# Placing score maxima, positive parts and splits in the projection stage by booked engine clocks instead of counted columns

## The chip, the cores and the metric

The kernel runs on one core of a Trainium2 chip. The metric is the device time of one execution, in microseconds (us). A core has TensorE (PE: matrix products, with its weight loads shown as PEld), VectorE (DVE), ScalarE (ACT), GpSimd (POOL) and SyncE (SP, which here only issues DMAs). Each engine works through its own queue in order and waits at an instruction until the semaphores that it needs have been raised. TensorE writes to PSUM, eight banks of 512 float32 columns on 128 partitions.

## The reference

One transformer block on 2048 tokens of 640 values, with 32 heads of 20 values, in float32:

```python
x = A_x
h = x + _A_ref(_layernorm(x), A_wqkv, A_wo)     # attention: softmax(q k^T * 20**-0.5) v, times wo
h2 = h + _B_ref(_layernorm(h), B_w_gate, B_w_up, B_w_down)   # (silu(z @ w_gate) * (z @ w_up)) @ w_down
```

The softmax subtracts the row maximum of the scores, so that maximum has to be known before the exponentials.

## The kernel before

The kernel has three stages. The first (the subject here) takes the layernorm of x, multiplies by wqkv, stores queries, keys and values in HBM, and computes a part of the score maxima ahead of the attention. The second is the attention with the remaining maxima, the third the output projection and the feed-forward part. All products are made in float32 precision from two reduced-precision parts: each operand is split into `hi` and `lo` (`split`, L84: ScalarE copies the value to `hi`, another engine subtracts), and three products hi*hi, lo*hi and hi*lo are summed.

**Work of the first stage.** Tokens come in four chunks of 512 (`c`). Each chunk has 10 query and key blocks (`query_key`, 512 columns wide) and 8 value blocks (`value`, 320 columns wide); `slot` counts them, 18 to a chunk, from 0 to 71. A block is the sum of 15 products (three kinds by five pieces of the 640 inner values). `rounds` (L484) issues each of these as two half matmuls on 64 of TensorE's 128 rows; the first half of one block runs at the same time as the second half of an older one, on the other rows. The second halves stand in the list `behind`: when it holds more than 21, the oldest is issued. Both halves add into the same bank, so after the last first half of a block a marker on VectorE (`clobber_nop`) has to pass before the first of its second halves may start. When a block's last second half is issued, `keep` (L546) or `keep_value` (L596) takes the bank: ScalarE copies it, the split follows, by `split_later` some columns later (ScalarE's copy and GpSimd's subtraction), and the result is stored to HBM by `store` (L469), from GpSimd's queue in most slots. `store` keeps the newest pieces back until the next call, a block later.

**Maxima between the blocks.** `max_pair` (L171) multiplies 128 queries by 512 keys for two heads (two matmuls, two banks) and VectorE reduces each bank to its maximum (L181). `max_four` (L185) does four heads with two reductions only. For two keys a and b, max(a, b) is b plus the positive part of a - b. The stored keys hold the differences of their halves as a third part, so `differences` multiplies the queries by key differences (four matmuls of 256 columns, two banks), ScalarE takes the positive part in place (Relu, L203), and `maxima` adds the products with the plain keys on top (four more matmuls) and VectorE reduces the sums (L208). Such a pair is called a job here. The tiles that a job reads (`raw`, six buffers) are loaded back from HBM by `load_items` (L319) on SP's queue, from a slot on at which the store has been issued (`stored_at`); `ready` (L347) lets a job go some slots after its load was issued. Banks for maxima (`ps_max`) rotate through five, block sums (`ps_one`) through three.

**What sets the order.** Every engine's queue is written out by this program; nothing is reordered later. `visit` (L389) is called after each product of a block, from slot 7 on, and decides whether a job goes in. It counts columns of TensorE work: a job's `maxima` comes `BEHIND` columns after its `differences`, and jobs are spaced by `BETWEEN` and `SPACING`:

```python
BETWEEN, SPACING, BEHIND = 11 * CH // 2, 5 * CH, 13 * CH // 2
```

Jobs stand in two lists, `early` (four heads, staged tiles) and `urgent` (maxima of the first unit, from tiles that stay); `early` goes first up to slot 59. The layernorm of the next chunk (`norm`, L429: statistics, an inverse root in small steps, application, all on VectorE) is taken apart into 15 steps, in the list `lns`, one or two of which are issued after each block. `flip` (L446) transposes the normalized chunk on TensorE. When the blocks are done, the rest of `behind` is issued with a `visit` after each; the maxima of unit 0 are finished by `max_finish` (L236), which the attention needs.

Of the kernel before, what the change touches and what calls it, by code (L numbers as in the profile page):

```python
# [17 lines left out]
P = 128  # L18
# [26 lines left out]
def tile_block(ctx: ExitStack, tc: tile.TileContext, x, wqkv, wo, wg, wu, wd, out):  # L45
# [123 lines left out]
    mxs = {u: stk.tile([P, 2, 2, TPC, NC], F32, name=f"mx{u}") for u in range(NU)}  # L169

    def max_pair(mx, q, k, pair, t, kc, k0):  # L171

        banks = [ps_max() for _ in range(2)]
        for b, ps in enumerate(banks):
            rows = slice(b * ROW, b * ROW + NPART)
            nc.tensor.matmul(  # L176
                ps, q[rows, pair, t * P : (t + 1) * P], k[rows, pair, k0 : k0 + CH],
                start=True, stop=True,
            )
        for b, ps in enumerate(banks):  # L180
            nc.vector.tensor_reduce(  # L181
                mx[:, b, pair, t, kc : kc + 1], ps, axis=AX.X, op=ALU.max
            )

    def max_four(mx, q, k, t, kc):  # L185
# [4 lines left out]
        def products(cols, first):  # L190
            for pair in range(2):
                for b in range(2):
# [5 lines left out]
                    )  # L198

        def differences():  # L200
            products(slice(half, CH), True)
            for ps in banks:
                nc.scalar.activation(ps, ps, AF.Relu)  # L203

        def maxima():
            products(slice(0, half), False)
            for b, ps in enumerate(banks):
                nc.vector.tensor_reduce(  # L208
                    mx[:, b, :, t, kc], ps.rearrange("p (j n) -> p j n", j=2),
                    axis=AX.X, op=ALU.max,  # L210
                )
# [73 lines left out]
    with tc.tile_pool(name="pa", bufs=2) as pa:  # L285
# [33 lines left out]
        def load_items():  # L319
            for n, (which, g, c, loaded, _) in enumerate(items):  # L320
# [10 lines left out]
                stack(t, which, g, c, slice(CH // 2, EW) if which else slice(0, CH))  # L331
                items[n][3:] = t, slot[0]

        def staged_keys(g, c, kc, k, q):
            def four(t):
                first, second = max_four(mxs[g * NC + c], items[q][3], items[k][3], t, kc)

                def last():
                    second()
                    for n in (k, q):  # L340
                        users[n] -= 1
                    load_items()

                first()
                return last

            def ready():  # L347
                return all(items[n][3] is not None and slot[0] >= items[n][4] + 2 + (slot[0] < 24) for n in (k, q))

# [35 lines left out]

        columns, due, seconds = [0], [0], []
        BETWEEN, SPACING, BEHIND = 11 * CH // 2, 5 * CH, 13 * CH // 2

        def visit():  # L389

            load_items()
            if seconds and columns[0] >= seconds[0][0]:
                columns[0] += CH
                seconds.pop(0)[1]()
            if columns[0] < due[0]:
                return
            for queue in (early, urgent) if slot[0] < 60 else (urgent, early):
                if queue and queue[0][0]():
                    columns[0] += CH
                    last = queue.pop(0)[1]()  # L400
                    if last:
                        seconds.append((columns[0] + BEHIND, last))
                    due[0] = max(due[0] + BETWEEN, columns[0] + SPACING)
                    return
            due[0] = max(due[0], columns[0] - 4 * BETWEEN)

# [12 lines left out]
        def split_w(m):  # L419
            cs = slice(m * P, (m + 1) * P)  # L420
            split(raws.pop(m), w_hi[:, :, cs], w_lo[:, :, cs])

        def z_tiles(c):
# [22 lines left out]
        def flip(c, k):  # L446
            if k == 0:
                zs[c] = z_tiles(c)
            ps = ps_max()
            for t in range(TPC):  # L450
                nc.tensor.transpose(  # L451
# [22 lines left out]

        behind, splits = [], []

        def second_half():
            if behind:
                f, done = behind.pop(0)
                f(1)  # L480
                if done:
                    done()

        def rounds(ps, n_columns, operands, done):  # L484

            last = len(operands) - 1
            for n, (a, b) in enumerate(operands):

                def half(i, n=n, a=a, b=b):
# [17 lines left out]

# [15 lines left out]

        def split_later(f):
            splits.append((columns[0] + 7 * CH, f))

# [19 lines left out]
        def keep(c, m, ps):  # L546

            finish_splits()
            e = next_e()
            which, half, n = 1 - m % 2, CH // 2, CH  # L550
# [3 lines left out]
            if slot[0] < 10:  # L554
                if which:
# [3 lines left out]
                    )  # L559
                split(ps, hi[:, :CH], lo[:, :CH], nc.vector)  # L560
                if which:
                    split_later(lambda: split(over, hi[:, CH:], lo[:, CH:], nc.gpsimd))
            else:
                nc.scalar.activation(copy[:, :CH], ps, AF.Copy)
                if which and c < 2:
# [30 lines left out]
        def keep_value(c, t, half, ps):  # L596
            finish_splits()
            ev = evs[t % 2]
            dst = ev[:, half * 4 : half * 4 + 4, : G * VW].rearrange("p g (h w) -> p g h w", h=G)
# [41 lines left out]
        for c in range(NC):  # L641
# [7 lines left out]
            for j, (kind, *which) in enumerate(work):  # L649
# [27 lines left out]
                else:  # L677
                    ps_ctx.close()
                    ps_ctx = ExitStack()
                    psum = ps_ctx.enter_context(  # L680
                        tc.tile_pool(name="psum_p", bufs=1, space=bass.MemoryType.PSUM)
                    )

                    def ps_one():
                        return psum.tile([P, CH], F32, name="ps_one", tag="ps_one", bufs=3)

                    def ps_max():
                        return psum.tile([P, CH], F32, name="ps_max", tag="ps_max", bufs=5)

# [1084 lines left out]
```

## Time and profile before

| | us |
|---|---|
| median of 3 runs (lowest, highest) | 2088.42 (2087.58, 2092.59) |
| the profiled execution | 2087.61 |
| its span, first to last instruction | 2085.5 |
| TensorE busy in the span | 2049.9 |
| VectorE busy | 1642.5 |
| ScalarE busy | 1440.5 |
| GpSimd busy | 744.3 |
| end of the last projection matmul, from the start of the span | 372.1 |

The span lies 2.1 us below the profiled execution's time; the rest is before its first and after its last instruction. In the rows below, a name like `ps_max<-raw,raw` tells the tile that is written and those that are read, L194 the line of the program, x4 that four instructions are merged, and `[0.51 <-DVE mx L208]` that the engine stood idle for 0.51 us before the row and what ended that. Rows of windows give, for each engine, the time it was busy in the stretch and the number of its instructions, then the granted TensorE clock as a share of full speed, the share of the DMA engines and GB/s. Rows of waits give who waited for whom, the sum in us, the count and the longest. Rows of grouped instructions give the count, busy us and mean ns of one, and after the second bar the idle time of the engine ahead of them. A busy TensorE is not one at its peak: overlapping matmuls, one of which is held up, count as busy.

### The profile page before, as it was taken

How to read it: one execution, taken by the hardware profiler on the slowest of the kernel's cores; microseconds unless marked ns; L12 is line 12 of the kernel's file. 1: busy time of each engine (PE TensorE's matmuls, PEld its weight loads, DVE VectorE, ACT ScalarE, POOL GpSimd, SP SyncE). 2: the span in 40 equal slices, each digit the busy share in tenths (PEclk: the TensorE clock that was granted, in tenths of full speed). 3: DMA queues.
4: the chain of work that ended last, by engine and by line, in shares of the span. 5: the costliest groups of instructions: out<-in, count | busy, mean ns of one | idle time of the engine just before them, and what ended most of it. 6: DMA issues, size and time to landing. Idle time of an engine off the chain costs nothing.

```text
span 2085.5 us, 39669 instructions
## 1 busy us (share of the span) xinstructions
PE 2049.9 (98%) x14198; PEld 1251.5 (60%) x14198; DVE 1642.5 (79%) x2895; ACT 1440.5 (69%) x2835; POOL 744.3 (36%) x1039
## 2 busy tenths in 40 slices
PE   7989999999999999999999999999999999999999
PEld 6878788433333433333333333335588888888888
DVE  6757878798888888888888888886368676676667
ACT  3657774899999999999999999996743222212221
POOL 2353423334342434353510001001145444753556
PEclk9999999999999999999999999999999999999999
DMA  6766553253354443534521213131138755884542
GB/s 216 234 205 187 180 162 107 64 159 109 128 155 128 140 125 122 168 124 154 177 100 58 52 32 98 31 117 61 35 123 291 249 182 176 307 300 156 196 155 95
DMA packets 192300, 305.53 MB, mean 146 GB/s; under 512 B 47440, under 2 KB 82256, under 8 KB 191080
## 3 DMA queue, kind: packets, MB, share of 16 engines
q1 hardware_dynamic: 185576, 278.87, 41.6%
q0 software_dynamic: 6432, 24.12, 3.8%
q8 instruction: 113, 1.85, 0.4%
q14 instruction: 83, 0.68, 0.1%
q10 hardware_dynamic: 96, 0.00, 0.0%
HBM read 203.82 MB, written 98.30 MB: 145 GB/s over the span
## 4 chain that ended last, share of the span: by engine, by line
PE 91%; DMA 4%; DVE 2%; issue 1%; ACT 1%; SPq 1%; POOL 0%; DVEq 0%; ACTq 0%; POOLq 0%
PE acc L1076 24%; PE ps_one L1066 16%; PE ps_a L1237 14%; PE ps_max L219 12%; PE ps_one L491 9%; PE ps_b L1331 7%; PE ps_max L194 4%; PE ps_max L797 2%; PE ps_b L797 1%; DVE mx L208 1%; DMA halves<-j_d 1%; DMA raw<-q_d 1%; DMA t<-t_d 1%; PE ps_max L451 0%; PE ps_max L176 0%
## 5 line engine op out<-in xcount | busy, mean ns | idle before, releaser
L1072 ACT ACTIVATE probs<-ps_one 128x512 f32<-128x512 f32 x2048 | 1056.8, 616 | 62.7 <-PE ps_one L1066 38.5
L225 DVE TENSOR_REDUCE mx<-ps_max 128x1 f32<-128x512 f32 x1472 | 925.7, 683 | 115.2 <-PE ps_one L1066 77.1
L1066 PE MATMUL ps_one<-q_stk,k_stk 62*128 62x512 f32 x2048 | 585.5, 450 | 2.6 <-DVE m L86 1.8
L1076 PE MATMUL acc<-probs,v_stk 128*32 128x512 f32 x4096 | 545.7, 605 | 0.0
L1066 PEld LDWEIGHTS ps_one<-q_stk,k_stk 62*128 62x128 f32 x2048 | 251.5, 184 | 432.4 <-ACT probs L1072 397.8
L219 PE MATMUL ps_max<-k_stk,q_stk 60*128 60x512 f32 x1472 | 382.6, 425 | 0.0
L219 PEld LDWEIGHTS ps_max<-k_stk,q_stk 60*128 60x128 f32 x1472 | 271.8, 186 | 24.7 <-DVE mx L225 1.1
L1452 DVE TENSOR_TENSOR tmp<-ps_a,tmp 128x512 f32<-128x512 f32 x208 | 141.1, 689 | 120.5 <-PE ps_a L1237 94.7
L208 DVE TENSOR_REDUCE mx<-ps_max 128x2 f32<-128x512 f32 x256 | 164.7, 686 | 67.9 <-PE ps_max L194 51.7
L1111 POOL TENSOR_TENSOR o<-o,rb 128x512 f32<-128x512 f32 x31 | 40.0, 1290 | 407.8 <-DMA q_stk<-q_d 174.1
L1076 PEld LDWEIGHTS acc<-probs,v_stk 128*32 128x32 f32 x4096 | 80.5, 108 | 173.8 <-issue 165.3
L1331 PE MATMUL ps_b<-halves,yp 128*128 128x320 f32 x1032 | 179.3, 308 | 1.9 <-DMA halves<-j_d 1.4
L1331 PEld LDWEIGHTS ps_b<-halves,yp 128*128 128x128 f32 x1032 | 165.1, 188 | 18.5 <-POOL yp L86 1.5
L203 ACT ACTIVATE ps_max<-ps_max 128x512 f32<-128x512 f32 x256 | 137.2, 579 | 55.5 <-PE ps_max L194 52.1
L1237 PE MATMUL ps_a<-t,units 128*128 128x512 f32 x624 | 162.5, 396 | 0.0
L1237 PE MATMUL ps_a<-z,units 128*128 128x512 f32 x516 | 133.8, 394 | 0.0
L86 POOL TENSOR_TENSOR yp<-y,yp 128x256 fp32r<-128x256 f32 x96 | 60.2, 627 | 188.0 <-ACT yp L85 188.0
L1237 PEld LDWEIGHTS ps_a<-t,units 128*128 128x128 f32 x624 | 112.6, 188 | 18.6
L491 PE MATMUL ps_one<-z_hi,w_hi 64*128 64x512 f32 x380 | 117.7, 407 | 3.8 <-DVE z_lo L86 2.5
L491 PE MATMUL ps_one<-z_lo,w_hi 64*128 64x512 f32 x380 | 117.7, 404 | 0.0
L491 PE MATMUL ps_one<-z_hi,w_lo 64*128 64x512 f32 x380 | 115.4, 400 | 0.0
L1336 DVE TENSOR_TENSOR h<-ps_b,h 128x320 f32<-128x320 f32 x248 | 109.9, 480 | 6.8 <-PE ps_b L1331 5.4
(201 smaller groups left out, 2699.7 us busy)
## 6 DMA issues: line engine op xcount, KB each, us to landing
units<-w_d SPq DMA_DIRECT2D x186, 256.0 KB
w_d<-stage SPq DMA_DIRECT2D x106, 256.0 KB
halves<-j_d SPq DMA_DIRECT2D x70, 320.0 KB
j_d<-stage SPq DMA_DIRECT2D x42, 320.0 KB
k_stk<-k_d SPq DMA_DIRECT2D x64, 160.0 KB
q_stk<-q_d SPq DMA_DIRECT2D x64, 160.0 KB
raw<-k_d SPq DMA_DIRECT2D x54, 160.0 KB
rb<-r_d SPq DMA_DIRECT2D x32, 256.0 KB
```

The lines of the kernel that those rows point to most:

```text
L203: nc.scalar.activation(ps, ps, AF.Relu)
L208: nc.vector.tensor_reduce(mx[:, b, :, t, kc], ps.rearrange("p (j n) -> p j n", j=2), axis=AX.X, op=ALU.max,)
L219: nc.tensor.matmul(ps, queries[u][rows, pair, t * P : (t + 1) * P], keys[u // NC][rows, pair, kc * CH : (kc + 1) * CH], start=True, stop=True,
L225: nc.vector.tensor_reduce(mxs[u][:, b, pair, t, kc : kc + 1], ps, axis=AX.X, op=ALU.max)
L491: nc.tensor.matmul(ps, a[rows], b[rows], start=(i == n == 0), stop=(i == 1 and n == last), skip_group_check=True,)
L1066: nc.tensor.matmul(ps, keys[u // NC][rows, p, kt * P : (kt + 1) * P], queries[u][rows, p, :], start=True, stop=True,)
L1072: nc.scalar.activation(probs[p][:, b, :], ps, AF.Exp, scale=scale)
L1076: nc.tensor.matmul(acc[32 * j : 32 * j + 32, :], values[u // NC][:, kt, j * VW : j * VW + 32], probs[j // 2][:, j % 2, :], start=(kt == 0) ...
L1237: nc.tensor.matmul(ps.rearrange("p (t n) -> p t n", t=TPC), w[k][:, i], z[k][:, :, j], start=(first and m == 0), stop=(last and m == len(n ...
L1331: nc.tensor.matmul(ps, a, b, start=(n == 0), stop=(n == len(pairs) - 1))
L1336: nc.vector.tensor_tensor(out=h, in0=ps, in1=h, op=ALU.add)
L1452: add = lambda out, ps, x: nc.vector.tensor_tensor(out=out, in0=ps, in1=x, op=ALU.add)
```

## The change

The column counts are replaced by four clocks in ns, one for each engine, kept while the program is written. `takes` books work on an engine: the work starts at that engine's clock or when its input is ready, whichever is later. `held` is the list of times at which the five maxima banks come free.

- A job's `differences` books 240 on PE and two Relus of 478 on ACT; its `maxima` goes when PE's clock has reached the end of the Relus plus 150, and books two reductions of 600 on DVE, which set when its two banks come free.
- `visit` starts a new job only when PE's clock has reached the time at which the second of the next two banks comes free and ACT's clock is no more than 500 ahead. It also issues a waiting split when its time has come and ACT is no more than 200 ahead, and (from slot 9 on) a norm step when DVE is no more than 100 ahead. It is called in every slot.
- Loads count as landed 8000 of PE's clock after `load_items` issued them (12000 up to slot 23), instead of two or three slots later.
- In most slots a block's store is issued right after its split instead of at the next block.
- Second halves follow after 19 instead of 21 products. `urgent` goes first from slot 57 instead of 60.
- The five and three banks come from two pools instead of one. The last loop also runs while jobs are left, and `max_finish` follows the loop if it has not been issued.

```diff
+    clock = dict.fromkeys(("PE", "ACT", "DVE", "POOL"), 0)
+    held = [[0] for _ in range(5)]
+    RELU = 150
+
+    def takes(engine, ns, ready=0):
+        clock[engine] = max(clock[engine], ready) + ns
+        return clock[engine]
+
+    def hold(*until):
+        held[: len(until)] = []
+        held.extend(until)
...
     def max_pair(mx, q, k, pair, t, kc, k0):
...
+        done = takes("PE", 240)
         for b, ps in enumerate(banks):
             nc.vector.tensor_reduce(
                 mx[:, b, pair, t, kc : kc + 1], ps, axis=AX.X, op=ALU.max
             )
+            hold([takes("DVE", 600, done + 205) + 100])
...
+        until = [[1e9] for _ in banks]
+
         def differences():
             products(slice(half, CH), True)
+            done = takes("PE", 240)
             for ps in banks:
                 nc.scalar.activation(ps, ps, AF.Relu)
+                takes("ACT", 478, done + 150)
+            hold(*until)
+            return clock["ACT"] + RELU
 
         def maxima():
             products(slice(0, half), False)
+            done = takes("PE", 240)
             for b, ps in enumerate(banks):
+                until[b][0] = takes("DVE", 600, done + 205) + 100
...
-                items[n][3:] = t, slot[0]
+                items[n][3:] = t, clock["PE"] + (LANDING if slot[0] > 23 else LANDING_FIRST)
...
-                return all(items[n][3] is not None and slot[0] >= items[n][4] + 2 + (slot[0] < 24) for n in (k, q))
+                return all(items[n][3] is not None and clock["PE"] >= items[n][4] for n in (k, q))
...
-        columns, due, seconds = [0], [0], []
-        BETWEEN, SPACING, BEHIND = 11 * CH // 2, 5 * CH, 13 * CH // 2
+        seconds, steps_due = [], [0]
+        LANDING, LANDING_FIRST, SLACK, GATE = 8000, 12000, 0, 500
 
         def visit():
 
             load_items()
-            if seconds and columns[0] >= seconds[0][0]:
-                columns[0] += CH
+            pe = clock["PE"]
+            if seconds and seconds[0][0] <= pe + SLACK:
                 seconds.pop(0)[1]()
-            if columns[0] < due[0]:
                 return
-            for queue in (early, urgent) if slot[0] < 60 else (urgent, early):
+            if splits and splits[0][0] <= pe and clock["ACT"] <= pe + 200:
+                splits.pop(0)[1]()
+            if steps_due[0] and lns and clock["DVE"] <= pe + 100:
+                steps_due[0] -= 1
+                lns.pop(0)()
+            if held[1][0] > pe + SLACK or clock["ACT"] > pe + GATE:
+                return
+            for queue in (early, urgent) if slot[0] < 57 else (urgent, early):
                 if queue and queue[0][0]():
-                    columns[0] += CH
                     last = queue.pop(0)[1]()
                     if last:
-                        seconds.append((columns[0] + BEHIND, last))
-                    due[0] = max(due[0] + BETWEEN, columns[0] + SPACING)
+                        seconds.append(last)
                     return
-            due[0] = max(due[0], columns[0] - 4 * BETWEEN)
...
+            takes("DVE", 750, takes("ACT", 590, clock["PE"]) + 100)
...
+            done = takes("PE", 850, held[0][0])
+            hold([takes("ACT", 478, done + 200) + 130])
+            takes("ACT", 478)
...
+        LAG = 19
+        given = [0, 0, 0]
 
         def second_half():
             if behind:
-                f, done = behind.pop(0)
+                f, crossed, done = behind.pop(0)
+                clock["PE"] = max(clock["PE"], crossed[0])
                 f(1)
                 if done:
                     done()
 
+        def taken(columns):
+            return takes("ACT", 46 + 0.844 * columns, clock["PE"] + 350) + 150
+
         def rounds(ps, n_columns, operands, done):
 
             last = len(operands) - 1
+            crossed = [0]
+            clock["PE"] = max(clock["PE"], given.pop(0))
...
                     if (i, n) == (0, last):
                         nc.vector.clobber_nop([nc.vector.lower_ap(ps)])
+                        crossed[0] = takes("DVE", 60, clock["PE"] + 450) + 50
 
                 half(0)
-                behind.append((half, done if n == last else None))
-                if len(behind) > 21:
+                takes("PE", 5 + 0.4427 * n_columns)
+                behind.append((half, crossed, done if n == last else None))
+                if len(behind) > LAG:
                     second_half()
-                columns[0] += n_columns
-                if slot[0] > 6:
-                    visit()
-                while splits and columns[0] >= splits[0][0]:
-                    splits.pop(0)[1]()
+                visit()
...
-        def split_later(f):
-            splits.append((columns[0] + 7 * CH, f))
+        def split_later(f, ready):
+
+            def late():
+                f()
+                takes("ACT", 600, ready)
+
+            splits.append((ready, late))
...
             finish_splits()
+            given.append(taken(CH))
...
-                split_later(lambda n=n: split(copy[:, :n], hi[:, :n], lo[:, :n], nc.gpsimd))
+
+                def finish(n=n):
+                    split(copy[:, :n], hi[:, :n], lo[:, :n], nc.gpsimd)
+                    if not sync:
+                        store()
+
+                split_later(finish, given[-1] + (700 if n > CH else 0))
...
-            store(*pieces, queue=nc.sync if sync else nc.gpsimd)
+            store(queue=nc.sync if sync else nc.gpsimd)
+            stores.extend(pieces)
...
-                for _ in range(2 if j >= 5 else 1):
-                    if j >= 1 and lns:
+                if slot[0] < 9:
+                    for _ in range(2 if j >= 5 else 1):
+                        if j >= 1 and lns:
+                            lns.pop(0)()
+                else:
+                    while steps_due[0] and lns:
+                        steps_due[0] -= 1
                         lns.pop(0)()
+                    steps_due[0] = 2 if j >= 4 else 1
...
-        while behind:
+        while behind or early or urgent or seconds:
             second_half()
-            columns[0] += CH
+            takes("PE", 150)
             visit()
-        finish_splits()
+            if not behind:
+                finish_splits()
+                slot[0] += 1
         store(queue=nc.sync)
-        print("left", len(urgent), len(early))
+        if 0 in ends:
+            max_finish(0)
```

More of the change, by code (lines that the diff above doesn't have):

```diff
@@ L342, in last @@
                     load_items()
-                first()
-                return last
+                return first(), last
             def ready():
-                return all(items[n][3] is not None and slot[0] >= items[n][4] + 2 + (slot[0] < 24) for n in (k, q))
+                return all(items[n][3] is not None and clock["PE"] >= items[n][4] for n in (k, q))
             ts = moved(g * NC + c, kc)
@@ L473, in store @@
             stores.extend(last)
-        behind, splits = [], []
+        behind, splits, lns = [], [], []
+        LAG = 19
+        given = [0, 0, 0]
         def second_half():
             if behind:
-                f, done = behind.pop(0)
+                f, crossed, done = behind.pop(0)
+                clock["PE"] = max(clock["PE"], crossed[0])
                 f(1)
@@ L560, in keep @@
                 split(ps, hi[:, :CH], lo[:, :CH], nc.vector)
+                given[-1] = takes("DVE", 1000 if which else 650, takes("ACT", 478) + 100) + 100
                 if which:
-                    split_later(lambda: split(over, hi[:, CH:], lo[:, CH:], nc.gpsimd))
+                    split_later(lambda: split(over, hi[:, CH:], lo[:, CH:], nc.gpsimd), given[-1] + 300)
             else:
@@ L597, in keep_value @@
             finish_splits()
+            given.append(taken(HALF))
             ev = evs[t % 2]
@@ L679, in tile_block @@
                     ps_ctx = ExitStack()
-                    psum = ps_ctx.enter_context(
-                        tc.tile_pool(name="psum_p", bufs=1, space=bass.MemoryType.PSUM)
+                    psum, psum_jobs = (
+                        ps_ctx.enter_context(
+                            tc.tile_pool(name=name, bufs=n, space=bass.MemoryType.PSUM)
+                        )
+                        for name, n in (("psum_p", 5), ("psum_j", 3))
                     )
                     def ps_one():
-                        return psum.tile([P, CH], F32, name="ps_one", tag="ps_one", bufs=3)
+                        return psum_jobs.tile([P, CH], F32, name="ps_one", tag="ps_one")
                     def ps_max():
-                        return psum.tile([P, CH], F32, name="ps_max", tag="ps_max", bufs=5)
+                        return psum.tile([P, CH], F32, name="ps_max", tag="ps_max")
                 if c == 0 and j == 6:
```

## The prediction

> **What bounds the kernel now.** I read the stage windows first, to see which engine is full in which stage.
>
> ```profile
> core 0: us, PE busy (x) PEld busy (x) DVE busy (x) ACT busy (x) POOL busy (x), PEclk, DMA share, GB/s
> 0.00:372.40 372.40, 347.05 (x3335) 291.06 (x3335) 262.86 (x474) 222.89 (x419) 131.02 (x156) 0.98 0.59 184
> 372.40:1412.00 1039.60, 1037.39 (x7227) 411.15 (x7228) 923.40 (x1529) 1008.65 (x1988) 299.47 (x462) 1.00 0.37 111
> 1412.00:2085.50 673.50, 665.43 (x3638) 549.29 (x3636) 456.26 (x892) 208.99 (x431) 313.85 (x421) 1.00 0.53 180
> ```
>
> The change lies in the first 372.4 us. What follows (1713.1 us) issues the same work from both programs and is full on TensorE, and in the middle on ScalarE (1008.65 of 1039.60). So what the projections win or lose should reach the end one for one.
>
> In the first stage TensorE looks 93% busy. That is misleading, so the chain of waits gives what a matmul costs when nothing holds it:
>
> ```profile
> 118.81 8.86 PE ps_one L491 x74
> ...
> 173.11 0.88 PE ps_one L491 x12
> ...
> 363.52 8.58 PE ps_one L491 x50
> ```
>
> 74 half matmuls in 8.86 us are 0.239 us for a pair of 512 columns; 12 in 0.88 us are 0.147 us for a pair of 320. The program issues 570 and 480 such pairs: 570 x 0.239 + 480 x 0.147 = 207 us. The stage's time beyond that goes to jobs (the 128 four-head maxima of two products each, and 32 pairs of plain maxima) and to waits. The list of waits from 20 to 372 us names them:
>
> ```profile
> ACT ps_max L203 <- PE ps_max L194: 52.1, 69, 5.6
> DVE mx L208 <- PE ps_max L194: 51.7, 100, 1.8
> ...
> PEld ps_max L194 <- DVE mx L208: 31.2, 75, 1.5
> ...
> PE ps_max L194 <- DVE mx L208: 5.1, 12, 1.2
> ...
> PE ps_max L194 <- DMA raw<-q_d: 4.5, 2, 2.5
> ```
>
> TensorE waits 31.2 + 5.1 = 36.3 us, 87 times, for VectorE to free a PSUM bank, yet VectorE in the same stretch waits 51.7 us for TensorE. So neither is the limit: they wait for each other in turn. The timeline shows one such turn:
>
> ```profile
> 217.81 0.50 PE L194 MATMUL ps_max<-raw,raw 60*128 60x256 f32 x3 [0.51 <-DVE mx L208]
> 218.03 0.40 PE L491 MATMUL ps_one<-z_lo,w_hi 64*128 64x512 f32 x1
> ...
> 218.24 1.07 ACT L203 ACTIVATE ps_max<-ps_max 128x512 f32<-128x512 f32 x2 [0.32 <-PE ps_max L194]
> 218.27 0.51 PE L194 MATMUL ps_max<-raw,raw 60*128 60x256 f32 x4
> 218.51 0.39 PE L491 MATMUL ps_one<-z_lo,w_hi 64*128 64x512 f32 x1
> ...
> 218.78 1.29 DVE L208 TENSOR_REDUCE mx<-ps_max 128x2 f32<-128x512 f32 x2 [0.43 <-PE ps_max L194]
> ...
> 219.53 0.29 PEld L194 LDWEIGHTS ps_max<-raw,raw 60*128 60x128 f32 x3 [0.36 <-DVE mx L208]
> ...
> 219.95 1.07 ACT L203 ACTIVATE ps_max<-ps_max 128x512 f32<-128x512 f32 x2 [0.64 <-PE ps_max L194]
> ...
> 220.50 1.29 DVE L208 TENSOR_REDUCE mx<-ps_max 128x2 f32<-128x512 f32 x2 [0.43 <-PE ps_max L194]
> ```
>
> A product costs 0.24 us (218.27 to the next projection matmul at 218.51). At 219.53 the next job's product is already at the head of TensorE's queue and stands 0.36 us; projection matmuls behind it, which need nothing, stand too. In that time VectorE and ScalarE run dry (0.43 and 0.64 us).
>
> VectorE would allow a shorter stage:
>
> ```profile
> 196.00:260.00 64.00, 59.73 (x576) 48.51 (x573) 51.88 (x99) 47.34 (x89) 22.56 (x29) 1.00 0.59 180
> ...
> 324.00:346.00 22.00, 22.00 (x268) 21.48 (x267) 20.20 (x32) 5.33 (x12) 7.11 (x10) 1.00 0.35 107
> ...
> sum 224.40, PE 218.20 PEld 185.56 DVE 166.90 ACT 148.83 POOL 80.44; mean PE 31.17 PEld 26.51 DVE 23.84 ACT 21.26 POOL 11.49
> ```
>
> From 148 to 372.4 us it works 166.9 of 224.4 us. With 30 us gone it would be 166.9 / 194.4 = 86% full, which the second row (20.20 of 22.00, 92%, with TensorE never idle) shows to be possible.
>
> **The change, part by part.** No engine's count of computing instructions changes; places do.
>
> *Jobs by clocks instead of columns.* I counted, in both programs' written order, how much TensorE work stands between a job's last product and the reuse of its bank five banks later (pairs at 0.239 and 0.147, products at 0.24, a four-transposition flip at 0.85 us, an estimate). Before, 104 of 315 reuses stand closer than 1.25 us, with a tenth at 1.02 or below; after, none, and 5 closer than 1.4. The wait on a 1.02 distance is the 0.36 us of the row at 219.53, so a bank needs about 1.38 us. Nearly all of the 36.3 us should go; a late start of VectorE will leave some. I take 90%: -32.8 us (ends: -36.3, and -18 if half stay).
>
> The price lies at the other edge. From a job's first product to its second the median distance falls from 1.90 to 1.67 us; 18 of 128 are below 1.5, 34 below 1.6. Needed are 0.24 (product) + 0.21 (218.03 to 218.24) + 1.07 (both Relus) = 1.52 us. ScalarE can be late by an evacuation:
>
> ```profile
> L203 ACT ACTIVATE ps_max<-ps_max 128x512 f32<-128x512 f32 x256 | 137.2, 579 | 55.5 <-PE ps_max L194 52.1 <-PE ps_one L491 0.5
> ...
> L121 DVE BATCH_NORM_STATS2 st<-xt 128x6 f32<-128x320 f32 x24 | 10.6, 483 | 9.5 <-PE ps_one L491 6.0 <-DMA raw<-in_A_wqkv 3.4
> ...
> L435 DVE TENSOR_SCALAR xt<-xt,mv,r_a 128x640 f32<-128x640 f32 x12 | 9.7, 827 | 0.1
> ...
> L564 ACT ACTIVATE e<-ps_one 128x512 f32<-128x512 f32 x20 | 12.0, 600 | 13.4 <-PE ps_one L491 6.3 <-DMA k_d<-e 3.9 <-issue 1.7
> ```
>
> The booked clock includes evacuations and splits, so I take 0.1 us on the 34 close ones: +4 us (ends: 0, and 0.3 us on half of the 128 jobs, +19).
>
> *LAG 21 to 19.* Two fewer lone halves when the pipeline fills and drains (the x50 row: 14.5 pairs and 21 lone halves, 35.5 x 0.239 = 8.5 us): 4 half slots of 0.12, -0.5 us. But a block's second halves wait for a VectorE marker behind its last first half. The distance for this falls at the median from 2.27 to 1.56 us (512 columns, 38 blocks) and from 1.58 to 1.28 us (320, 32 blocks). Behind the marker's waiter stand all matmuls of the queue. The work of two reductions (1.29 us) and a matmul's 0.39 us can stand ahead of the marker, so some crossings will wait; the trace has no such wait now. I take 0.04 us for each of 70: +3 us (ends: 0, and the slower rival below).
>
> *The load wait.*
>
> ```profile
> 136.20:141.10 4.90, 0.55 (x1) 0.28 (x1) 0.73 (x4) 0.02 (x1) 3.85 (x6) 0.75 0.92 258
> 141.10:146.00 4.90, 4.84 (x30) 4.74 (x30) 0.73 (x2) 2.64 (x5) 0.00 (x0) 0.55 0.85 262
> ```
>
> ```profile
> 138.68 0.55 PE L194 MATMUL ps_max<-raw 60*128 60x256 f32 x1 [2.55 <-DMA raw<-q_d]
> 141.16 0.77 PE L194 MATMUL ps_max<-raw 60*128 60x256 f32 x3 [1.93 <-DMA raw<-q_d]
> ```
>
> The first job on the second token block waits 2.55 + 1.93 us for its tiles, and for 4.9 us afterwards the granted clock is 0.55, which costs 4.9 x 0.45 = 2.2 us. After the change this job stands 6 pairs later (311.5 instead of 305.5 column pairs) with two pairs of plain maxima before it: 6 x 0.239 + 2 x 0.24 = 1.9 us. GpSimd's queue has each store right behind its split, where now the next block's subtraction comes first, so SP's queue, where the load waits for the store, moves sooner. I take -4.5 of the 6.7 us (ends: 0 and -6.7).
>
> The Trainium skill (TensorE: Matmul & The Clock Gate, What's actually happening) says that an idle window of about 3.4 us halves the clock until a busy window has passed; the trace agrees, with 4.9 us at 0.55. By its window the slow spell would cost 1.7 instead of 2.2 us, and the sum would be 0.5 us smaller.
>
> *Norm steps, splits, the urgent queue first from slot 57, pools.* The pools keep 5 + 3 banks. Splits and norm steps keep their engines (VectorE 86% full, ScalarE less); their cover is the slack just named, and without it the clocks' omission of norm steps is the third rival. Three short stores move from SP's queue to GpSimd's, which works 131.02 of 372.40 us: nothing.
>
> *The tail.* Jobs now reach the last 30 pairs (10 reductions instead of 2), so the attention's first banks may wait for one job's reductions: +1 us (ends 0 and 1.8, its two Relus or reductions late).
>
> Sum: -32.8 + 4 - 0.5 + 3 - 4.5 + 1 = -29.8 us. The profiled execution took 2087.61 us (span 2085.5 and 2.1 around it), 0.8 below the median of 2088.42: 2087.6 - 29.8 = 2058 us.
>
> **The rivals.**
>
> *1. The wait changes its releaser.* ScalarE's Relus hold the second product as the banks held the first. For it: the distance shrank to 1.67 against a need of 1.52. Against it: the 52.1 us that the Relus wait for TensorE show ScalarE free. With +19 for +4 the gain is 15: 2073 us (2068 to 2081).
>
> *2. Slower: the crossings.* If VectorE's queue holds a job's two reductions at each crossing, a second half needs 0.39 + 1.29 = 1.68 us from the last first half and waits 0.12 (at 1.56) or 0.40 (at 1.28): 38 x 0.12 + 32 x 0.40 = 17 us, still faster. With two jobs in the queue (2.97 us) it waits 1.41 or 1.69: 108 us, 2163. It decides from 0.47 us at each of the 70 (33 us, against the gain of 33 without the 3 booked); I set its time between these ends and near the lower, with a wait of 0.6 us: 2087.6 - 33 + 42 = 2097 us. Against it: from 324 to 346 us VectorE is 92% full, the blocks are of 320 columns, whose smallest distances now are 1.34 us, and TensorE stands nowhere. For it: everything behind the marker stands still, as at 219.53.
> The Trainium skill (the same page, The mechanism) has matmuls start and end strictly in order, so no other row group passes a waiting one; the row at 219.53 agrees.
>
> *3. The clocks do not track the engines.* VectorE's clock books no norm step. Two token blocks' worth (16 x 0.483 + 8 x 0.827, and 28 short steps and 8 aggregations of some 0.2 us, an estimate: 21 us) come on top unseen. If each turned into a bank wait and the Relus took half of their upper end, 30 - 21 - 6 leaves 3 us: 2085 us, no change.
>
> **How the numbers follow.** Forecast: 0.62, from 2044 (every named wait gone: -36.3 - 6.7 - 0.5 = -43.5) to 2068 (a third of the bank waits stay). Below that, where better places save TensorE time that no wait names: 0.05. Rival 1, with part of 3: 0.15. Rival 3 whole: 0.06. Rival 2: 0.12. About 6 us (0.3%) is what a measurement of this kernel can tell from no change. Faster: 0.62 + 0.05 + 0.15 = 0.82; same 0.06; slower 0.12. The range 2042 to 2081 holds the forecast, some of the lower case and rival 1, about 0.8. The forecast's own range is 2044 to 2068.
>
> **What would show it.** Right: the projections end near 343 us instead of 372; TensorE's waits for the reductions fall from 36.3 to under 8 us; waits of the second product on Relus stay under 8 us; the 2.55 and 1.93 us for raw tiles mostly go and the clock stays near 1.00 around 140 us; VectorE is near 85% full from 148 us on. Wrong: waits of TensorE released by ScalarE's Relus of 15 us or more (rival 1); projection matmuls released by VectorE at the starts of second halves, 20 us or more (rival 2); bank waits that stay, clustered at norm steps (rival 3); or an attention stage that grows by what the projections gave.

## The result and the profile after

The changed kernel takes 2072.85 us (median of 4 runs, 2072.07 to 2073.68) against 2088.0 (4 runs, 2085.85 to 2092.59): a ratio of 0.9925, with a 95% interval of 0.9907 to 0.9942. That is 15.2 us less. The forecast was 2058 us: it is faster as forecast, with half of the gain. The time lies inside the stated range (2042 to 2081 us), but outside the forecast's own (2044 to 2068), in the part that was left to the first rival.

The stage windows of the changed kernel (same columns as before; the first row now ends where the projections end):

```profile
core 0: us, PE busy (x) PEld busy (x) DVE busy (x) ACT busy (x) POOL busy (x), PEclk, DMA share, GB/s
0.00:357.00 357.00, 329.47 (x3335) 297.57 (x3335) 260.05 (x474) 219.06 (x419) 131.97 (x158) 0.97 0.61 192
```

The 3335 matmuls of the first stage are done by 357.0 instead of 372.4 us, and the span fell from 2085.5 to 2070.1 us: 15.4 in both. What the projections gave arrived at the end one for one.

Its waits from 20 to 372 us:

```profile
DVE mx L230 <- PE ps_max L208: 48.3, 58, 2.1
ACT ps_max L220 <- PE ps_max L208: 41.2, 42, 7.1
...
PEld ps_max L208 <- DVE mx L230: 8.9, 4, 6.0
...
PE ps_max L208 <- DVE mx L230: 7.4, 2, 5.7
...
DVE st L121 <- DMA xt<-in_A_x: 6.3, 1, 6.3
...
PEld ps_max L208 <- ACT ps_max L220: 3.7, 9, 1.1
...
PE ps_one L527 <- ACT e L605: 2.5, 2, 1.8
```

The many short waits of the product for the reductions (31.2 us in 75) have become 8.9 us in 4, of which one is 6.0. The products' wait for raw tiles fell from 4.5 to 0.5 us. One name is new: VectorE waits once for the load of x. A projection matmul waits for ScalarE's copy 2.5 us in two, where it waited 0.8 us once.

Of the signs that the prediction named, two held (Relu waits of 3.7 us, hardly any wait for raw tiles). The projections end halfway (357.0, not 343 us), the waits for reductions are 8.9 us instead of under 8, the clock from 132 to 148 us is 0.89, and VectorE is 77% busy from 148 us to the projections' end (160.95 of 209.0 us) instead of 85%.

The clearest view is one stretch in which both kernels issue the same projection matmuls. These two rows count those alone: first the kernel before, 205.5 to 259.5 us, then the changed one, 203.8 to 243.5 us:

```profile
205.50:259.50 54.00, 43.67 (x249) 29.17 (x247) 1.00 0.58 176
```

```profile
203.80:243.50 39.70, 39.65 (x249) 28.86 (x245) 1.00 0.68 208
```

The same 249 half matmuls take 39.7 instead of 54.0 us. The products of jobs in these stretches are 234 and 190 matmuls:

```profile
205.50:259.50 54.00, 36.76 (x234) 28.00 (x234) 1.00 0.58 176
```

```profile
203.80:243.50 39.70, 24.35 (x190) 24.26 (x190) 1.00 0.68 208
```

These are 124.5 pairs, with 58.5 products before and 47.5 after. In the second stretch the list of waits has none of TensorE; in the first it has this one and, inside it, 2.9 us of the matmuls themselves:

```profile
PEld ps_max L194 <- DVE mx L208: 13.1, 29, 0.8
```

By the prices of the prediction the second stretch would take 124.5 x 0.239 + 47.5 x 0.24 = 41.2 us; it took 39.7, so with nothing waiting a pair or product costs 39.7 / 172 = 0.231 us. At that price the first stretch has 183 x 0.231 = 42.2 us of work, and 11.8 of its 54.0 us were waiting. The remaining 2.5 us of the difference are the 11 products that the changed kernel does later. The timeline of the second stretch shows the placement, with no idle time listed ahead of a product:

```profile
220.32 2.05 ACT L220 ACTIVATE ps_max<-ps_max 128x512 f32<-128x512 f32 x4 [0.43 <-PE ps_max L208]
...
220.82 0.40 PE L208 MATMUL ps_max<-raw,raw 60*128 60x256 f32 x3
...
221.52 0.40 PE L208 MATMUL ps_max<-raw,raw 60*128 60x256 f32 x3
...
222.04 2.49 DVE L230 TENSOR_REDUCE mx<-ps_max 128x2 f32<-128x512 f32 x4
...
222.46 0.40 PE L208 MATMUL ps_max<-raw,raw 60*128 60x256 f32 x3
```

Four Relus and four reductions now run in one piece each (2.05 and 2.49 us), where they ran two by two before.

A good part of the expected gain was given back in single places. The largest, in the timeline of the changed kernel from 100 us on:

```profile
99.83 2.22 SPq L316 DMA_DIRECT2D xt<-in_A_x  x3
...
106.35 0.89 DVE L121 BATCH_NORM_STATS2 st<-xt 128x6 f32<-128x320 f32 x2 [6.27 <-DMA xt<-in_A_x]
...
108.10 0.50 PEld L208 LDWEIGHTS ps_max<-raw,raw 60*128 60x128 f32 x3 [6.04 <-DVE mx L230]
108.10 0.79 PE L208 MATMUL ps_max<-raw,raw 60*128 60x256 f32 x3 [5.72 <-DVE mx L230]
108.72 0.58 ACT L220 ACTIVATE ps_max<-ps_max 128x512 f32<-128x512 f32 x1 [7.14 <-PE ps_max L208]
```

A layernorm statistic of the third chunk stands at the head of VectorE's queue for 6.27 us until x has landed. The reductions behind it cannot pass, so no bank comes free, and TensorE stands for 5.72 us. The windows add what follows:

```profile
102.40:108.10 5.70, 0.00 (x1) 0.00 (x2) 1.72 (x5) 0.00 (x0) 0.00 (x0) 0.79 0.88 259
108.10:112.00 3.90, 3.90 (x26) 3.85 (x28) 3.83 (x10) 2.14 (x4) 0.00 (x0) 0.50 0.00 1
112.00:116.00 4.00, 4.00 (x42) 3.79 (x40) 3.10 (x6) 2.58 (x5) 0.00 (x0) 0.94 0.00 0
```

After the idle time the clock is 0.50 for 3.9 us and 0.94 for 4.0: 1.95 + 0.24 = 2.2 us more. By this estimate the place costs 5.7 + 2.2 = 7.9 us. The Trainium skill (TensorE: Matmul & The Clock Gate, What's actually happening) gives half the clock until a busy window of about 3.4 us has passed; the trace agrees, with 0.50 over 3.9 us.

The second, from 134 us on:

```profile
138.17 1.69 POOL L500 DMA_DIRECT2D k_d<-v_stk  x3 [0.30 <-POOL v_stk L86]
139.88 0.74 POOL L607 TENSOR_TENSOR e<-e 128x256 f32<-128x256 f32 x1
...
140.65 0.84 ACT L85 ACTIVATE e<-e 128x768 fp32r<-128x768 f32 x1 [4.24 <-POOL e L607]
141.40 0.58 ACT L605 ACTIVATE e<-ps_one 128x512 f32<-128x512 f32 x1
...
142.03 0.50 PE L527 MATMUL ps_one<-z_hi,w_hi 64*128 64x512 f32 x1 [1.81 <-ACT e L605]
```

This is the moved store: GpSimd issues it (1.69 us) ahead of the next block's subtraction (L607), ScalarE's split waits 4.24 us for that, its copy of the block behind stands with it, and TensorE waits 1.81 us for the bank. The clock then falls here too, which costs another 3.4 x 0.50 = 1.7 us:

```profile
143.20:146.60 3.40, 3.40 (x23) 2.79 (x21) 3.35 (x5) 0.09 (x1) 2.67 (x4) 0.50 0.84 268
```

### The profile page after: what moved, and what is told of

It is laid out like the page before. It is cut to its first block, busy times and chain, and to the rows that moved or that the text cites. A ratio compares the mean times of both kernels' runs of the same rounds, so it can differ in the third digit from the quotient of the medians.

```text
span 2070.1 us, 39666 instructions
## 1 busy us (share of the span) xinstructions
PE 2031.9 (98%) x14198; PEld 1257.6 (61%) x14198; DVE 1637.2 (79%) x2895; ACT 1437.0 (69%) x2835; POOL 745.3 (36%) x1042
## 3 DMA queue, kind: packets, MB, share of 16 engines
q1 hardware_dynamic: 185272, 278.34, 42.2%
## 4 chain that ended last, share of the span: by engine, by line
PE 89%; DMA 4%; DVE 3%; POOL 1%; ACT 1%; issue 1%; SPq 1%; ACTq 0%; DVEq 0%; POOLq 0%
PE acc L1137 25%; PE ps_one L1127 16%; PE ps_a L1298 15%; PE ps_max L241 12%; PE ps_b L1392 8%; PE ps_one L527 7%; PE ps_max L208 2%; PE ps_max L858 2%; PE ps_b L858 1%; DMA halves<-j_d 1%; DVE mx L194 1%; DMA q_d<-e 1%; DMA xt<-in_A_x 1%; DMA units<-w_d 0%; DMA k_d<-v_stk 0%
## 5 line engine op out<-in xcount | busy, mean ns | idle before, releaser
L220 ACT ACTIVATE ps_max<-ps_max 128x512 f32<-128x512 f32 x256 | 135.8, 581 | 47.4 <-PE ps_max L208 41.2
L527 PE MATMUL ps_one<-z_hi,w_hi 64*128 64x512 f32 x380 | 108.9, 410 | 5.7 <-DVE z_lo L86 2.9
L527 PE MATMUL ps_one<-z_hi,w_lo 64*128 64x512 f32 x380 | 108.8, 402 | 0.0
L527 PE MATMUL ps_one<-z_lo,w_hi 64*128 64x512 f32 x380 | 108.1, 405 | 0.0
```

The source lines that it names most:

```text
L527: nc.tensor.matmul(ps, a[rows], b[rows], start=(i == n == 0), stop=(i == 1 and n == last), skip_group_check=True,)
```

## The experiments

Every kernel ran beside the kernel before; the times are medians, and ratios are to the kernel before. Runs of one kernel spread by 2 to 8 us and the intervals of most changed kernels overlap, so differences of a few us between two experiments are read from the traces rather than from the medians.

**The count of norm steps that is left over.** In the changed kernel `steps_due` is 2 when a chunk's list is empty, and stays 2, so the next chunk's first two statistics are issued in the very slot that issues the load of x.

```diff
                     lns = norm(c + 1)
+                    steps_due[0] = 0
```

> Theory (a): part of the expected gain is lost in one place, from 100 to 112 us, where two layernorm statistics of the third chunk stand at the head of VectorE's queue 6.27 us for the load of x, with the reductions behind them, because the count of steps due is left at 2 from the chunk before and they are issued in the very slot that issues the load. With the count set to 0 when a new list of steps is made, this wait and the slow clock behind it should go: some 8 us less than the changed kernel, 2065 us (2063 to 2067). Theory (b), the missing gain is spread over many small waits of second products and crossings: 2072 to 2073 us, no change.

Measured: 2068.6 us (ratio 0.9911, 0.9894 to 0.9927), the span 2066.5 us. From its waits:

```profile
PEld ps_max L208 <- DVE mx L230: 4.2, 4, 2.6
...
DVE st L121 <- DMA xt<-in_A_x: 3.2, 2, 2.5
...
PE ps_max L208 <- DVE mx L230: 2.7, 2, 2.2
...
PEld ps_max L208 <- ACT e L320: 2.0, 1, 2.0
```

(a) held for half of its 8 us: the median is 4.3 us lower than that of the changed kernel, the span 3.6 us. The statistic comes a slot later and still waits 2.5 us. A product's wait for ScalarE's copy of a transposed chunk (L320) is 2.0 instead of 1.2 us.

**All norm steps by slot again.**

```diff
-            if steps_due[0] and lns and clock["DVE"] <= pe + 100:
-                steps_due[0] -= 1
-                lns.pop(0)()
...
-                if slot[0] < 9:
-                    for _ in range(2 if j >= 5 else 1):
-                        if j >= 1 and lns:
-                            lns.pop(0)()
-                else:
-                    while steps_due[0] and lns:
-                        steps_due[0] -= 1
-                        lns.pop(0)()
-                    steps_due[0] = 2 if j >= 4 else 1
+                for _ in range(2 if j >= 5 else 1):
+                    if j >= 1 and lns:
+                        lns.pop(0)()
```

> All layernorm steps are placed as before the change, one or two at the end of each slot from the chunk's second slot on; jobs, splits and stores by the clocks. If theory (a) holds and steps placed by VectorE's clock also hurt at 190 to 200 us (three statistics in a row ahead of reductions, TensorE waits 1.63 us): 2062 to 2065 us. If placing steps by the clock is worth something elsewhere, less is gained than by the reset alone: 2066 to 2070 us. If the steps do not matter: 2073 us.

Measured: 2068.22 us (0.9902, 0.9887 to 0.9917), the span 2065.8. Waits for the load of x are gone. In their place TensorE waits longer for Relus, and for key tiles:

```profile
PEld ps_max L208 <- ACT ps_max L220: 4.9, 7, 2.1
...
PEld ps_max L208 <- DVE mx L230: 3.0, 6, 1.1
...
PE ps_max L208 <- DMA raw<-k_d: 1.2, 2, 0.9
```

The time is that of the reset. So placing norm steps by VectorE's clock is worth nothing measurable against fixed slots, once they do not stand ahead of their load.

**The load of x a slot earlier**, on top of the reset:

```diff
                 if j == 0 and c + 1 < NC:
-                    if c > 0:
-                        load_x(c + 1)
                     lns = norm(c + 1)
...
+                if j == 17 and c + 2 < NC:
+                    load_x(c + 2)
```

> With the reset, and the loads of x for the third and fourth chunk issued one slot earlier (the last slot of the chunk before, behind the last transposition that reads the buffers). Theory (a): VectorE's wait for xt, 3.2 us left with the reset, goes, and with it TensorE's waits of up to 2.6 us: 2064 to 2067 us against 2068.6. If the wait that is left there is covered: 2068 to 2069 us.

Measured: 2066.54 us (2063.78 to 2071.76; 0.9896, 0.9866 to 0.9925), the span 2061.8 in the trace, which is that of the run of 2063.78 us. It is the lowest median of all, but the interval overlaps with that of the reset. VectorE's wait for x is 2.3 us in one, TensorE's longest wait for a reduction 2.3 us; the direction is that of (a), the wait is not quite gone. So no experiment wins back all of the 7.9 us: this one wins 6.3 by the medians. That the wait for x costs time is clear all the same: the 12 runs of the three kernels that shorten or remove it (2063.78 to 2071.95 us) all lie below the four of the changed kernel.

**The stores held back again** (the rest as changed):

```diff
-                    if not sync:
-                        store()
...
-            store(queue=nc.sync if sync else nc.gpsimd)
-            stores.extend(pieces)
+            store(*pieces, queue=nc.sync if sync else nc.gpsimd)
```

> Stores go back to being held until the next block; the rest is as changed. Theory (c): a store issued right behind its split stands ahead of the next block's subtraction on GpSimd's queue, ScalarE waits for that with the next split (4.24 us at 140 us), and TensorE for ScalarE's copies (0.69 and 1.81 us): without it some 3 us less, 2070 us. Theory (d): the earlier stores are what lets the tiles of the second chunk land in time; then TensorE's wait for raw<-q_d (4.5 us before the change, none after) comes back and the time is 2076 to 2079 us.

Measured: 2073.82 us (0.9931, 0.9917 to 0.9946), not faster. Its waits:

```profile
PE ps_max L208 <- DMA raw<-q_d: 3.2, 1, 3.2
ACT e L85 <- POOL e L607: 2.5, 3, 0.8
```

Both mechanisms are there. ScalarE's wait for GpSimd falls from 8.8 to 2.5 us and TensorE's wait for ScalarE's copy is no longer among the rows, as (c) had it; but 3.2 us for raw tiles return, as (d) had it. The moved store trades one wait for another; the time lies between those that (c) and (d) gave, and the two kernels' times cannot be told apart.

**Late stores with a longer landing time**, with the reset: loads issued in slots 18 to 23 count as landed after 15000.

```diff
-                items[n][3:] = t, clock["PE"] + (LANDING if slot[0] > 23 else LANDING_FIRST)
+                items[n][3:] = t, clock["PE"] + (LANDING if slot[0] > 23 else 15000 if slot[0] > 17 else LANDING_FIRST)
```

> Reset, stores held until the next block as before the change, and loads that are issued in slots 18 to 23 count as landed after 15000 instead of 12000. Holding the stores took away ScalarE's wait for GpSimd at 140 us, but the tiles landed later (3.2 us of waiting for raw<-q_d). If both waits can be avoided together (jobs 3 us later, with projection matmuls in their place): 2063 to 2066 us against 2068.6 with the reset alone. If the later jobs are missing in VectorE's time at the end: 2068 us or more.

Measured: 2068.07 us (0.9904, 0.9889 to 0.9919), no gain over the reset: 2.8 us for raw tiles and, in one piece, 3.5 us for `q_stk` remain. The trace is that of the run of 2072.65 us; the other three took 2068.05 to 2068.07, so the longest of these waits need not stand in them.

**Key stores by SyncE's queue**, with the reset, then with the earlier x as well:

```diff
                     if not sync:
-                        store()
+                        store(queue=nc.sync if n > CH else nc.gpsimd)
```

> With the reset, and the stores of the second chunk's key blocks, issued right behind their split as in the change, go through SyncE's queue instead of GpSimd's. Theory (c): GpSimd then takes the next subtraction at once, ScalarE's wait for it (8.7 us in three) and TensorE's for ScalarE's copies (2.4 us, and the slow clock behind) go: 2064 to 2066 us. If SyncE, held by the stores, lets the tile loads go later and TensorE waits for raw tiles instead: 2068 us or more.

> Reset, earlier loads of x and key stores by SyncE together. If both waits are separate the gains add: 2060 to 2064 us. If the waits only trade places with others, 2066 us or more.

Measured: 2073.26 us (0.9928, 0.9905 to 0.995) and 2072.05 us (0.9919, 0.9893 to 0.9945): 4.7 and 5.5 us slower than without by the medians, though the intervals overlap. In the first:

```profile
PE ps_max L208 <- DMA raw<-q_d: 6.1, 1, 6.1
```

ScalarE's wait for GpSimd falls to 2.6 us. But SyncE's queue, which issues the tile loads, now has the stores ahead of them: five stores take it 5.21 us from 123.50 us on, the first load of a raw key tile behind them is issued at 134.0 instead of 127.2 us (with the reset alone), and TensorE waits 6.1 us at once for tiles. The waits traded places.

**Norm steps booked on VectorE's clock**, on top of the last:

```diff
                 steps_due[0] -= 1
                 lns.pop(0)()
+                takes("DVE", 800, pe)
```

> As the one before, and each norm step that is placed by the clock books 800 ns on VectorE's clock. The third rival of the prediction in small: if unbooked steps cost bank waits (three statistics in a row at 195 us held TensorE 1.63 us), 1 to 3 us less than without. If not, the same time within 1 us.

Measured: 2077.9 us (0.9945, 0.9927 to 0.9962), slower by 5.9 than the one before. The waits show 7.2 us for `raw<-k_d`, 4.9 for x and one of 4.5 for a Relu. This settles little about unbooked steps: the kernel that it builds on has only 0.2 us of waits for reductions (3.5 in two, longest 3.3) besides the one behind the load of x, so booking had almost nothing to win there. Why booking brings these loads into the way was not followed further.

**The distance of second halves**, 21 as before the change, alone and with the reset:

```diff
-        LAG = 19
+        LAG = 21
```

> Only the distance of second halves goes back from 19 to 21. Theory (e), the slower rival of the prediction in small: second halves wait for VectorE's marker behind reductions at many of the 70 crossings; then the longer distance saves what they cost, 3 us or more: 2070 us or less. Theory (f): the crossings cost nothing, and two more lone halves at each end cost 0.5 us: 2073 to 2074 us.

> The count of norm steps is reset as in the first experiment and the distance of second halves is 21. Theory (f): the 6.5 us that 21 cost alone came from statistics that stood longer for their load (8.2 and 2.8 us instead of 6.3), not from TensorE; with the reset the two distances differ by the lone halves only: 2069 to 2070 us. Theory (g): 21 costs by itself, through jobs that are placed worse: 2073 us or more. Theory (e), crossings that wait at 19: 2066 us or less.

Measured: 2079.36 us (0.9958, 0.9944 to 0.9973) and 2072.0 us (0.9919, 0.9903 to 0.9936). VectorE's timeline of the first:

```profile
106.86 0.89 DVE L121 BATCH_NORM_STATS2 st<-xt 128x6 f32<-128x320 f32 x2 [8.22 <-DMA xt<-in_A_x]
```

The statistics wait 8.22 us there (and 2.78 us at 196 us), and 5.63 us with the reset; that the same clocks place them differently is presumably why. TensorE's matmuls wait 13.4 us for reductions instead of 7.4, where the kernel loses 6.5 us, and with the reset 8.4 instead of 2.7, where it loses 3.4. So the load of x is enough to account for what 21 costs. No time came out as (e), (f) or (g) gave it. Against (e) speaks the list of waits: the marker (L532) holds TensorE once, for 1.0 us of weight loads, with 19 as with 21.

**Can fixed counts do it?** The kernel before, with other numbers:

```diff
-        BETWEEN, SPACING, BEHIND = 11 * CH // 2, 5 * CH, 13 * CH // 2
+        BETWEEN, SPACING, BEHIND = 11 * CH // 2, 4 * CH, 9 * CH // 2
```

> The kernel before with its column counts, only SPACING 4 instead of 5 and BEHIND 4.5 instead of 6.5. Bank reuses closer than 1.25 us fall from 104 to 22 (closer than 1.4: 105 to 66), first to second product falls to 1.44 us at the median, with 54 of 128 below 1.5. Theory (h): what the change gains is the distance to the reuse of a bank, whoever sets it: waits for reductions fall by some 20 us, waits for Relus rise by 5 to 10: 2074 to 2078 us against 2087 before. Theory (i): the booked clocks gain because they follow each engine's load, and fixed counts with other numbers gain nothing: 2085 us or more.

and with `11 * CH // 2, 5 * CH, 7 * CH // 2`:

> The kernel before with BEHIND 3.5 instead of 6.5 alone. No bank is reused closer than 1.55 us, but 107 of 128 second products stand less than 1.3 us behind the first, against 1.52 needed. By the first rival of the prediction the wait changes its releaser: waits for reductions near 0, waits for Relus of 0.3 to 0.5 us at 107 jobs, 32 to 53 us: 2083 to 2104 us, no gain. If the second product need not wait so long (ScalarE starts earlier when nothing stands still): 2065 to 2075 us.

Measured: 2081.49 us (0.9964, 0.9953 to 0.9976) and 2101.56 us (1.0059, 1.0044 to 1.0074). The waits of the first:

```profile
PEld ps_max L194 <- ACT ps_max L203: 14.2, 54, 1.0
PEld ps_max L194 <- DVE mx L208: 10.8, 24, 2.4
```

and of the second:

```profile
PEld ps_max L194 <- ACT ps_max L203: 36.6, 127, 0.7
```

The first gains half of what the change gains: bank waits fall from 31.2 to 10.8 us, but 14.2 us of Relu waits come in. Its trace is that of a run of 2085.41 us, and has 7.1 us of waits for raw tiles where 4.5 stood. In the second the bank waits are nearly gone and 127 of 128 second products wait for their Relu, 0.29 us each. That is the first rival in pure form, and slower than before, as its expectation allowed. So distance sets the bank waits, whoever sets the distance, as (h) had it; its price for the Relus was too low, and so was its time. The first setting meets both edges, the second one of them; the clocks pass between (8.9 and 3.7 us). Other settings of the counts were not run, so it is not shown that only clocks can do this.

Sums of weight loads' waits are not time lost one for one: the 36.6 us here stand against 31.2 before, yet the kernel is 12.7 us slower.

## Why the prediction came out as it did

- *The mechanism* was right: TensorE, VectorE and ScalarE waited for each other in turn, and distance removed it. In the steady stretch the waits went from 11.8 us to none.
- *The bank waits, -32.8.* The term was too large at its start. The sum of 31.2 and 5.1 counts waits twice: a weight load (PEld) and its matmul (PE) stand for the same release, as the two rows at 108.10 us show. The term starts from 31.2; without the one wait of 6.0, 2.9 are left: -28.3. Even that is high, since in the steady stretch 13.1 us of such waits stood for 11.8 us lost.
- *Relus, +4:* 3.7 us in 9, where 0.3 stood before: +3.4. *Crossings, +3:* the marker held TensorE once, for 1.0 us of weight loads; the slower rival's price was never near. *Tail, +1:* nothing. The attention's first product waits 0.74 us for ScalarE's last copy (at 357.32 us), and it waited 0.74 us before the change (at 372.82 us).
- *The load wait, -4.5 of 6.7:* 4.0 of the 4.5 us went, but the moved store put 2.5 us of waits for ScalarE's copies in their place (0.8 before), and with them a slow clock that costs 1.7 us instead of 2.2: -4.0 + 1.7 - 0.5 = -2.8. That the earlier store delays the next subtraction was not seen, though the working named that order.
- *The step that failed: norm steps at nothing, "their cover is the slack just named".* Slack covers a step only if its input is there when its turn comes. The steps were counted as work of VectorE, not as a wait for a DMA with all reductions behind it: +7.9 us where 0 stood (5.7 us of waiting and, by the estimate above, 2.2 us of slow clock).
- *Not in the sum:* one product waits 1.2 us for ScalarE's copy of a transposed chunk (L320), one plain product 0.7 us for `q_stk`, and the plain maxima wait 4.3 us for reductions where they waited 2.7 (1.7 and 1.0), together +3.5:

```profile
PEld ps_max L188 <- DVE mx L194: 4.3, 9, 1.9
```

With these and the 0.5 us of lone halves as predicted (not measured by itself), the sum is -28.3 + 3.4 + 1.0 - 0.5 - 2.8 + 7.9 + 3.5 = -15.8 us against -15.4 measured in the span. The closeness is in part luck: the bank waits count somewhat too much, and waits too short for the list are in no term.

- *The rivals.* The time is that of the first rival (2073), its mechanism is not: Relu waits stayed at 3.7 us. That the time fell into the stated range through the room left for this rival is luck. The third had the right place, the norm steps, and mostly the wrong reason: their load held TensorE 5.72 us. A smaller wait is of its kind: at 198.0 us TensorE stood 1.63 us behind three statistics in a row (194.3 to 197.4 us) whose load had landed.

## What to carry to other kernels

When two engines both wait for each other by the list of waits, neither is full: count the distance, in the time of the waiting engine, between release and reuse on both edges, and move the work between them. A plan that moves steps by the load of engines must also know when each step's input lands, since one step at the head of an in-order queue holds every step behind it. Before adding up waits, see whether two rows stand for the same release.

## What was not expected of the hardware

A wait of TensorE costs more than itself where it is long: after 5.7 us the granted clock was 0.50 for 3.9 us, and after two waits of 2.55 and 1.93 us in the kernel before it was 0.55 for 4.9 us, while the 75 waits of 0.4 us left it at 1.00. It need not be as long as the idle window that the prediction cites: after the one wait of 1.81 us at 142.0 us the clock was 0.50 for 3.4 us, and in the run with the earlier load of x a wait of 2.03 us up to 105.3 us was followed by 0.50 from 105.8 to 109.2 us. The wait of 1.63 us at 198.0 us left it at 1.00.
